# One product's halves in another order, and two ring copies cut in two: a strided-attention and MLP kernel on Trainium2

## The chip, the cores and the metric

The kernel runs on one core of a Trainium2 chip. Its time is the device time of one execution in microseconds; lower is better. The engines go by these names in the profile: PE is TensorE's matmul, PEld its weight load, DVE is VectorE, ACT is ScalarE, POOL is GpSimd, SP is SyncE, which here only issues DMAs. A small q behind a name means that engine's instruction queue.

## The reference: what is computed

Two stages follow each other. The first is attention over 8 batches of 8 heads, 576 positions and 64 values per head, where the heads 0 to 3 see the last 32 positions and the heads 4 to 7 see every 32nd one. The second is an MLP with a leaky activation on the 4608 tokens that come out, with `d_model` 512 and `d_ff` 2048.

```python
scores = scale * np.matmul(q, k.transpose(0, 1, 3, 2))
mask_local = (rel >= 0) & (rel < stride)
mask_strided = (rel >= 0) & (pos[None, :] % stride == pos[:, None] % stride)
scores = np.where(masks[None, :, :, :], scores, -1000000000.0)
attn = softmax(scores)                      # written out in the reference
x = (attn @ v).transpose(0, 2, 1, 3).reshape(B * S, H * D)
h = x @ w_in
g = np.maximum(h, 0.0) + alpha * np.minimum(h, 0.0)
out = g @ w_out
```

## The kernel before, in words

**Tiles and stages.** The 4608 tokens of the MLP are taken in nine chunks of 512 (0 to 8). Attention works on batches of 576 tokens, two heads at a time (a pair: `hp` 0 and 1 are the local heads, 2 and 3 the strided ones). Its results go, transposed, into `xT`, a ring of 1536 columns for the 512 rows of x. A chunk reads 512 columns of the ring; a batch fills 576, so batches and chunks don't end together. Batch 7 fills columns 960 to 1535. Chunk 7 reads columns 512 to 1023, so it needs the first 64 columns of batch 7; chunk 8 reads columns 1024 to 1535.

**How a batch gets into the ring.** Local pairs of later batches go by a transposing DMA from SP's queue straight into `xT` (L446). The strided pair `hp` 2 goes by a transposing DMA into a tile `xs` (L443), and from there by a ScalarE copy that reorders the columns (`x_copy`, L452). The strided pair `hp` 3 is transposed on TensorE into a PSUM tile `xp` (L429) and copied by ScalarE in the same reordering (`x_piece`, L207). `spans` says into which stretches of the ring a batch goes: one, or two where it wraps.

**Layer 1.** For each of 16 groups of 128 rows of `d_ff`, four matmuls of 128x512 (L583) make `hps` in PSUM, in the order 2, 3, 0, 1 of the row blocks of x. ScalarE makes `neg` (L591), VectorE joins both to the activation `gT` (L594). Three PSUM banks are in use for these groups and for the banks of layer 2.

**Layer 2.** From chunk 2 on, the product of `gT` and `w_out` is made with seven products in place of eight (Winograd's form). The 512 tokens are split into two token halves, the columns of `w_out` into two halves, and the contraction over `d_ff` into pairs of 128-row blocks, even and odd. The kernel's products P1 to P7 are made in the order 1, 5, 6, 2, 7, 3, 4. Each is two runs of 8 matmuls of 128x256 (L708): run r makes the r-th 128 tokens of the product's 256, and its step y goes over the eight pairs of `d_ff`. P3, P5, P6 and P7 take sums `gsum` of the four parts of `gT`; P5 takes `gsum[0]`, P6 takes `gsum[1]`, which is made from `gsum[0]`. Each sum is made in two halves by L652: half 0 is pairs 0 to 3 (the first half of `d_ff`), half 1 is pairs 4 to 7. Half 0 of `gsum[0]` and of `gsum[2]` is made early on GpSimd, the rest on VectorE behind the last activations of the chunk. So steps 0 to 3 of P5 need GpSimd's half, and steps 4 to 7 need VectorE's.

**Order.** Every instruction is put out in program order on its engine. The loop at the end of the kernel steps through 30 pieces of a chunk (16 of layer 1, 14 of layer 2) and sets attention pieces of the next batch between them at an even rate. P5 is steps 2 and 3 of layer 2 (its runs r = 0 and r = 1), P6 steps 4 and 5. In chunk 8, the last, the second run of P5 has a PSUM bank of its own. In chunks 7 and 8 there is no attention left to do.

The wait for a sum is carried by the weight load of the first matmul that needs it; what stands behind that load on TensorE waits with it.

Of the kernel before, what the change touches and what calls it, by code (L numbers as in the profile page):

```python
# [32 lines left out]
def kernel(  # L33
# [10 lines left out]
    nc = tc.nc  # L44
    keep = tc.keep_in_program_order

    B, H, S, D = q.shape
# [24 lines left out]
    wsum = [cpool.tile([128, 8, 256], F16, name=f"wsum{i}") for i in range(4)]  # L72
    gsum = [cpool.tile([128, 8, 256], F16, name=f"gsum{i}") for i in range(4)]
# [131 lines left out]
    def cast_copy(eng, o, i):  # L205
        if eng == "act":
            keep(nc.scalar.copy(o, i))  # L207
        elif eng == "dve":
            keep(nc.vector.tensor_copy(o, i))
        else:  # L210
            keep(nc.gpsimd.tensor_copy(o, i))  # L211
# [205 lines left out]
            pvv[:, :, 0:64],  # L417
            rc[0:w, 0:nb].unsqueeze(2).to_broadcast([w, nb, 64]), op=ALU.mult))

    def spans(b):  # L420

        d0 = b * S % RING
        w = min(S, RING - d0)
        return [(0, d0, w)] + ([(w, 0, S - w)] if w < S else [])

    def x_piece(P, eng):
        xp = pspool.tile([128, 1024], F16, tag="ps", name="xp")
        for t in range(P.n):
            keep(nc.tensor.transpose(  # L429
                xp[:, P.w * t : P.w * t + P.w], P.x16[0 : P.w, 128 * t : 128 * t + 128], ident[0 : P.w, 0 : P.w]))  # L430
        for s0, d0, w in spans(P.b):
            o = xT[:, P.hp, d0 : d0 + w]
            if P.strided:
                cast_copy(
                    eng, o.rearrange("r (p t) -> r p t", t=8),
                    xp[:, 0:576].rearrange("r (t p) -> r p t", t=8)[:, s0 // 8 : (s0 + w) // 8, :])
            else:
                cast_copy(eng, o, xp[:, s0 : s0 + w])

    def x_dma(P):  # L440
        if P.strided:
            P.xs = xpool.tile([128, 8, 80], F16, tag="xs", bufs=2, name="xs")
            keep(nc.sync.dma_start_transpose(P.xs, P.x16[0:80, :]))  # L443
        else:
            for s0, d0, w in spans(P.b):
                keep(nc.sync.dma_start_transpose(  # L446
                    xT[:, P.hp, d0 : d0 + w].rearrange("r (w p) -> r w p", p=96),
                    P.x16[0:96, 128 * (s0 // 96) : 128 * ((s0 + w) // 96)]))

    def x_copy(P):  # L450
        for s0, d0, w in spans(P.b):
            keep(nc.scalar.copy(  # L452
                xT[:, P.hp, d0 : d0 + w].rearrange("r (p t) -> r p t", t=8),
                P.xs[:, :, s0 // 8 : (s0 + w) // 8].rearrange("r t p -> r p t")))
# [17 lines left out]
    def X(g, eng=None):  # L472
        return lambda: x_piece(pairs[g], eng or ("act" if pairs[g].strided else "dve"))

    for g in range(7, npair + 2):
# [30 lines left out]
        for i, (kind, fn) in enumerate(seq):  # L506
# [6 lines left out]
            def run(fn=fn, extra=extra, g=g, c=c, kind=kind, lastp=(i == lastP), first=(i == 0),  # L513
# [29 lines left out]
                if second and 4 * DX <= g - 3 < npair and pairs[g - 3].xd and pairs[g - 3].strided:  # L543
                    after.append(lambda: x_copy(pairs[g - 3]))
# [109 lines left out]
    def store(n, t, c, src, add=None, r=None):  # L654

        osb = opool.tile([128, 512], F32, tag="osb", name="osb")
        r0, o = 512 * n + 256 * t, osb
        if r is not None:
            r0, o, src, add = r0 + 128 * r, osb[:, 0:256], src[:, 0:256], add[:, 256 * r : 256 * r + 256]
        if add is None:  # L660
            keep(nc.scalar.copy(o, src))  # L661
        else:
            keep(nc.vector.tensor_tensor(o, src, add, op=ALU.add))  # L663
        dst = out[r0 : r0 + (256 if r is None else 128), 256 * c : 256 * c + 256]
        if r is None:
            dst, o = dst.rearrange("(r p) c -> p r c", p=128), o.rearrange("p (r c) -> p r c", r=2)
        keep(nc.sync.dma_start(dst, o))

    bank = {}

    def lin2_fast(n, i):

        last = n == NCH - 1
        x, r = (("1", i) if i < 2 else ("5", i - 2) if i < 4 else ("6", i - 4) if i < 6 else ("2", i - 6) if i < 8
                else ("7", i - 8) if i < 10 else ("3", i - 10) if i < 12 else ("4", i - 12))
        if last and i > 10:
            x, r = (("4", 0), ("4", 1), ("3", 1))[i - 11]  # L680
        b = {"1": "a", "2": "a", "5": "e", "3": "e"}.get(x, "b")
        first = x in "15" and r == 0
        if first:
            bank[b] = phpool.tile([128, 512], F32, tag="hps", name="ops")
        o = bank[b][:, 256 * r : 256 * r + 256]
        if last and b == "e" and r == 1:
            if x == "5":
                bank["f"] = pspool.tile([128, 512], F32, tag="ps", name="opsl")
                first = True
            o = bank["f"][:, 0:256]  # L690

        def g(t, j):
            return lambda y: gTs[n][:, 2 * y + j, 256 * t + 128 * r : 256 * t + 128 * r + 128]

        def s(z):
            return lambda y: gsum[z][:, y, 128 * r : 128 * r + 128]

        def w(j, c):
            return lambda y: wout16[:, 2 * y + j, 256 * c : 256 * c + 256]

        def t(z):
            return lambda y: wsum[z][:, y, :]

        lhs, rhs = {
            "1": (g(0, 0), w(0, 0)), "2": (g(0, 1), w(1, 0)), "3": (s(3), w(1, 1)),
            "4": (g(1, 1), t(3)), "5": (s(0), t(0)), "6": (s(1), t(1)), "7": (s(2), t(2))}[x]
        for y in range(8):
            keep(nc.tensor.matmul(  # L708
                o, lhs(y), rhs(y), start=(first and y == 0), stop=(y == 7), skip_group_check=True))
        if last and x == "3":  # L710
            store(n, 0, 1, bank["f" if r else "e"], bank["s6"], r)
            return
        if last and x == "5":
            if r == 0:
                bank["s5"] = npool.tile([128, 512], F32, tag="par", bufs=2, name="par")
            keep(nc.scalar.copy(bank["s5"][:, 256 * r : 256 * r + 256], o))
            return
        if r == 0:
            return
        if x == "1":  # L720
            bank["b"] = phpool.tile([128, 512], F32, tag="hps", name="ops")
            keep(nc.scalar.copy(bank["b"], bank["a"]))
        elif x in "56":
            z = npool.tile([128, 512], F32, tag="par", bufs=2, name="par")
            keep(nc.scalar.copy(z, bank[b]))  # L725
            bank["s" + x] = z
        elif x == "2":
            store(n, 0, 0, bank["a"])
        elif x == "7":
            late.append(lambda: store(n, 1, 1, bank["b"], bank["s5"]))  # L730
        elif x == "3":
            late.append(lambda: store(n, 0, 1, bank["e"], bank["s6"]))
        else:
            store(n, 1, 0, bank["b"])
# [173 lines left out]
    for n in range(1, NCH):  # L908
        ab = attn_until(n + 1) if n + 1 < B else len(pieces)
        left = ab - pos["i"]  # L910
        acc = -1.5 if n == 1 else 0.0
        for i in range(32 if n < FAST else 30):
            if i < 16:
                lin1_piece(n, i if n < FAST else 8 * (i // 8) + 2 * (i % 4) + i % 8 // 4)
            elif n < FAST:
                lin2_piece(n, i - 16)
            else:
                lin2_fast(n, i - 16)
            acc += left / (22 if n < FAST else 19.5 if n == B - 2 else 21) * (0.5 if i < 16 else 1.0)
            cnt = int(acc)  # L920
            acc -= cnt
            attn_n(cnt, ab)
            if n < FAST:
                if i in (18, 21, 24, 27):
                    wout_sum((i - 18) // 3)
                continue
            for z, h, eng in sums.get(i, ()):
                g_sum(n, z, h, eng)
        while pos["i"] < ab:
            attn_step(ab)  # L930
# [30 lines left out]
```

## Time and profile before

| what | value |
|---|---|
| time, median of 3 runs | 301.9 us (301.6 to 302.09) |
| the profiled execution's own time | 301.52 us |
| its span, first to last instruction | 299.7 us |
| granted TensorE clock, mean | 0.998 |
| TensorE matmul busy | 293.2 us (98%) |
| VectorE, ScalarE, GpSimd busy | 219.1, 178.6, 171.9 us |
| chunks 3, 4, 5 (123.6 to 214.6 us) | 30.3, 30.3, 30.4 us each |
| chunk 6 (214.6 to 243.8 us) | 29.2 us |
| chunk 7 (243.8 to 270.0 us) | 26.2 us |

All times inside an execution are counted from the start of the span. The profile's waits list an engine's idle time in front of an instruction and what ended it; idle times under 0.15 us are not listed. In a timeline row the first number is the start and the second the length, and a number behind x says how many instructions of a kind the row joins. A matmul's length is longer than the distance to the next one, because matmuls are pipelined. The chain that ended last is followed back from the last instruction: at each step to what released it, or to the instruction before it on its engine.

### The profile page before, as it was taken

Reading aid. Unit: us, or ns where it says so; the run is one execution under the profiler, and the core shown is the slowest. Engines: PE = TensorE matmul, PEld = TensorE weight load, DVE = VectorE, ACT = ScalarE, POOL = GpSimd, SP = SyncE. Lnnn points to the kernel's source line nnn. Section 1 sums busy time; section 2 is a strip of 40 time slices with the busy share of each in tenths; the row PEclk is TensorE's granted clock in tenths of the full one; section 3 lists DMA queues with packets and bytes.
Section 4 is the critical chain, followed back from the end, with each engine's and each line's share of the span. In section 5 each row is a group of like instructions: output and inputs, shape, how many; then the busy total and the mean of one; then the engine's idle time right before and its main releaser. Section 6 shows DMA issues by size and latency. Waiting matters only on the chain.

```text
span 299.7 us, 6824 instructions
## 1 busy us (share of the span) xinstructions
PE 293.2 (98%) x2683; PEld 181.8 (61%) x2683; DVE 219.1 (73%) x408; ACT 178.6 (60%) x330; POOL 171.9 (57%) x160
## 2 busy tenths in 40 slices
PE   8999999999999999999999999999999999999995
PEld 3754545554544478646864686468745964684584
DVE  5677886668775897588848984898489948926852
ACT  1676755698457765776477647764676356416730
POOL 8362270049969998979897987595563305002300
PEclk9999999999999999999999999999999999999999
DMA  7999999999996969999989999966811140022004
GB/s 184 257 191 199 241 211 264 198 209 298 115 204 133 113 101 102 177 178 125 132 147 181 139 150 163 208 95 95 193 22 21 24 140 0 2 72 70 0 2 141
DMA packets 96976, 41.18 MB, mean 137 GB/s; under 512 B 75360, under 2 KB 93232, under 8 KB 96944
## 3 DMA queue, kind: packets, MB, share of 16 engines
q0 software_dynamic: 51008, 17.77, 59.0%
q1 hardware_dynamic: 45584, 22.32, 35.1%
q10 hardware_dynamic: 352, 0.66, 0.9%
q8 instruction: 21, 0.34, 0.5%
q14 instruction: 11, 0.09, 0.1%
HBM read 38.24 MB, written 9.44 MB: 159 GB/s over the span
## 4 chain that ended last, share of the span: by engine, by line
PE 84%; DVE 7%; ACT 4%; issue 2%; DMA 2%; SPq 0%; DVEq 0%; ACTq 0%
PE hps L583 37%; PE ops L708 24%; PE ops L622 5%; PE pv L406 4%; PE ops L864 3%; DVE gsum L652 2%; DVE gT L594 2%; PE sp L353 2%; DMA consts<-consts 2%; ACT neg L591 1%; PE xp L429 1%; PE sph L353 1%; DVE x L415 1%; PE ops L879 1%; ACT et L382 1%
## 5 line engine op out<-in xcount | busy, mean ns | idle before, releaser
L583 PE MATMUL hps<-xT,win 128*128 128x512 f16 x576 | 131.9, 379 | 0.2 <-ACT xT L452 0.2
L594 DVE SCALAR_TENSOR_TENSOR gT<-neg,oma,hps 128x512 f16<-128x512 f32 x144 | 105.3, 744 | 36.5 <-ACT neg L591 28.4
L591 ACT ACTIVATE neg<-hps 128x512 f32<-128x512 f32 x144 | 85.8, 598 | 35.7 <-PE hps L583 33.7
L583 PEld LDWEIGHTS <-win 128*128 128x128 f16 x576 | 53.7, 98 | 59.2 <-issue 0.5
L652 POOL TENSOR_TENSOR gsum<-gT 128x1024 f16<-128x1024 f16 x14 | 29.7, 2123 | 42.2 <-DVE gT L594 37.2
L378 POOL TENSOR_TENSOR et<-et,consts 128x576 f16<-128x576 f16 (+1 forms) x24 | 34.7, 1446 | 30.7 <-ACT et L376 30.5
L708 PEld LDWEIGHTS <-gsum 128*128 128x128 f16 x448 | 40.9, 98 | 7.3 <-DVE gsum L652 1.9
L708 PE MATMUL ops<-wsum,gsum 128*128 128x256 f16 x328 | 41.6, 273 | 0.3
L708 PEld LDWEIGHTS <-gT 128*128 128x128 f16 x336 | 31.5, 98 | 5.4 <-issue 0.3
L415 DVE TENSOR_TENSOR x<-pv,rc 96x384 f16<-96x384 f32 (+2 forms) x62 | 33.0, 532 | 2.1
L385 POOL TENSOR_TENSOR et<-et,consts 128x576 f16<-128x576 f16 (+1 forms) x24 | 31.4, 1309 | 0.0
L406 PEld LDWEIGHTS <-et 72*128 72x128 f16 (+1 forms) x448 | 23.4, 98 | 11.4 <-issue 1.8
L708 PE MATMUL ops<-wout,gT 128*128 128x256 f16 x224 | 27.9, 273 | 0.1
L376 ACT ACTIVATE et<-sp 128x576 f16<-128x576 f32 (+1 forms) x24 | 15.5, 644 | 17.1 <-PE sp L353 17.1
L413 DVE RECIPROCAL rc<-pv 96x6 f32<-96x6 f32 (+2 forms) x80 | 14.7, 183 | 10.6 <-PE pv L406 10.4
L211 POOL COPY vs<-stv 72x1024 f16<-72x1024 f16 x12 | 13.3, 1115 | 15.2 <-DMA stv<-in_v_dram 15.2
L663 DVE TENSOR_TENSOR osb<-ops,par 128x512 f32<-128x512 f32 (+1 forms) x14 | 9.4, 673 | 16.1 <-PE ops L708 8.2
L382 ACT ACTIVATE et<-sph 128x288 f16<-128x288 f32 (+1 forms) x48 | 18.8, 409 | 0.0
L661 ACT COPY osb<-ops 128x512 f32<-128x512 f32 x14 | 8.2, 585 | 16.8 <-PE ops L708 16.7
L622 PE MATMUL ops<-wout,gT 128*128 128x512 f16 x64 | 16.4, 379 | 0.0
L406 PE MATMUL pv<-vs,et 72*128 72x65 f16 x256 | 15.4, 193 | 0.8 <-ACT qT L207 0.5
L725 ACT COPY par<-ops 128x512 f32<-128x512 f32 x13 | 7.6, 585 | 14.1 <-PE ops L708 14.1
(105 smaller groups left out, 331.8 us busy)
## 6 DMA issues: line engine op xcount, KB each, us to landing
out_dram<-osb SPq DMA_DIRECT2D x35, 256.0 KB, 4.0
vl<-in_v_dram POOLq DMA_DIRECT2D x6, 384.0 KB, 9.3
win<-in_moe_w_in_dram POOLq DMA_DIRECT2D x4, 512.0 KB, 17.6
wout<-in_moe_w_out_dram POOLq DMA_DIRECT2D x4, 512.0 KB, 15.6
qsd<-in_q_dram POOLq DMA_DIRECT2D x7, 288.0 KB, 6.2
ksd<-in_k_dram POOLq DMA_DIRECT2D x7, 288.0 KB, 7.6
stv<-in_v_dram POOLq DMA_DIRECT2D x7, 288.0 KB, 7.8
ql<-in_q_dram SPq DMA_DIRECT2D x3, 576.0 KB, 7.3
```

The lines of the kernel that those rows point to most:

```text
L376: keep(nc.scalar.activation(ev.rearrange("r (y c) -> r y c", y=2), sp[0:r, :, 0:n], AF.Exp, scale=SCALE))
L378: keep(nc.gpsimd.tensor_tensor(mv, mv, m, op=ALU.mult))
L382: keep(nc.scalar.activation(ev[:, n * y : n * y + n], sps[y][0:r, 0:n], AF.Exp, scale=SCALE))
L385: keep(nc.gpsimd.tensor_tensor(mv, mv, m, op=ALU.mult))
L406: keep(nc.tensor.matmul(pv[:, 65 * x : 65 * x + 65], et[0:r, c : c + 128], v16[0:r, 2 * P.pr + hh, t, :] if P.strided else v16[:, 6 * (2 * ...
L415: keep(nc.vector.tensor_tensor(P.x16[0:w, c0 : c0 + 64 * nb].rearrange("r (c e) -> r c e", e=64), pvv[:, :, 0:64], rc[0:w, 0:nb].unsqueeze ...
L583: keep(nc.tensor.matmul(hps, win16[:, kk, 128 * m : 128 * m + 128], xT[:, kk, c0 : c0 + 512], start=(kk == 2), stop=(kk == 1)))
L591: keep(nc.scalar.activation(neg, hps, AF.Relu, scale=-1.0))
L594: keep(nc.vector.scalar_tensor_tensor(gTs[n][:, m, :], neg, oma[:, m : m + 1], hps, op0=ALU.mult, op1=ALU.add))
L622: keep(nc.tensor.matmul(ops, gTs[n][:, kf, 128 * mt : 128 * mt + 128], wout16[:, kf, :], start=(kf == 0), stop=(kf == 15)))
L652: keep((nc.vector if eng == "dve" else nc.gpsimd).tensor_tensor(gsum[i][:, hs], a, b, op=op))
L708: keep(nc.tensor.matmul(o, lhs(y), rhs(y), start=(first and y == 0), stop=(y == 7), skip_group_check=True))
```

## The change

There are two parts.

1. P5 of the chunks 2 to 7. Before, run r = 0 goes through the steps 0 to 7 and then run r = 1 through the steps 0 to 7. After, the first of the two pieces takes the steps 0 to 3 of both runs, and the second the steps 4 to 7 of both. The matmuls are the same sixteen, into the same bank. Chunk 8 keeps the old order.
2. Batch 7's strided pairs. `spans` gets an argument; where it is set and the batch is the last, it gives two stretches, 64 and 512 columns long, in place of one of 576. So the copy from `xp` (L207) and the copy from `xs` (L452) become two each. The order on ScalarE is: 64 columns from `xp`, 512 from `xp`, 64 from `xs`, 512 from `xs`. Local pairs and other batches stay.

```diff
-    def spans(b):
+    def spans(b, cut=False):
 
         d0 = b * S % RING
+        if cut and b == B - 1:
+            return [(0, d0, 64), (64, d0 + 64, S - 64)]
         w = min(S, RING - d0)
         return [(0, d0, w)] + ([(w, 0, S - w)] if w < S else [])
...
-        for s0, d0, w in spans(P.b):
+        for s0, d0, w in spans(P.b, P.strided):
...
     def x_copy(P):
-        for s0, d0, w in spans(P.b):
+        for s0, d0, w in spans(P.b, True):
...
+        def both(h):
+            for z in range(2):
+                for y in range(4 * h, 4 * h + 4):
+                    keep(nc.tensor.matmul(
+                        bank["e"][:, 256 * z : 256 * z + 256], gsum[0][:, y, 128 * z : 128 * z + 128], wsum[0][:, y, :],
+                        start=(z == 0 and y == 0), stop=(y == 7), skip_group_check=True))
+
...
-        for y in range(8):
+        if x == "5" and not last:
+            both(r)
+        for y in range(8 if x != "5" or last else 0):
             keep(nc.tensor.matmul(
                 o, lhs(y), rhs(y), start=(first and y == 0), stop=(y == 7), skip_group_check=True))
```

## The prediction

> **What bounds the kernel now.** I read the page first (shares, the chain that ended last), then the table of waits, then the timeline around the waits that the change touches, at last single matmuls in windows of a tenth of a microsecond. The page says TensorE: it is busy for 98% of the span and holds 84% of the chain, so only its idle time can be won. The table of waits then names its two idle times that this change speaks of.
>
> ```profile
> PE 293.2 (98%) x2683; PEld 181.8 (61%) x2683; DVE 219.1 (73%) x408; ACT 178.6 (60%) x330; POOL 171.9 (57%) x160
> PE 84%; DVE 7%; ACT 4%; issue 2%; DMA 2%; SPq 0%; DVEq 0%; ACTq 0%
> PEld L708 <- DVE gsum L652: 1.9, 6, 0.4
> PE hps L583 <- ACT xT L452: 0.2, 1, 0.2
> ```
>
> The first wait is six stalls of the weight loads at P5's fifth matmul, where the second half of its sum is still being made on VectorE: once each in chunks 2, 3, 4, 5, 7 and 8 (chunk 6 has none). The second is the first matmul of chunk 7, which waits for the copy that fills the x ring.
>
> Chunk 3, the timeline of VectorE and of the weight loads (start, length, both us):
>
> ```profile
> 139.66 1.28 POOL L385 TENSOR_TENSOR et<-et,consts 72x576 f16<-72x576 f16 x1
> 140.40 1.10 DVE L652 TENSOR_TENSOR gsum<-gT 128x1024 f16<-128x1024 f16 x1
> 141.43 0.68 DVE L652 TENSOR_TENSOR gsum<-gsum,gT 128x1024 f16<-128x1024 f16 x1
> 142.72 0.68 DVE L652 TENSOR_TENSOR gsum<-gsum,gT 128x1024 f16<-128x1024 f16 x1
> ...
> 141.56 1.21 PEld L708 LDWEIGHTS <-gsum 128*128 128x128 f16 x12 [0.33 <-DVE gsum L652]
> ...
> 142.98 0.35 PEld L708 LDWEIGHTS <-gsum 128*128 128x128 f16 x4
> 143.45 0.11 PEld L708 LDWEIGHTS <-gsum 128*128 128x128 f16 x2
> ```
>
> The sums of VectorE come out at 141.50 (P5's second half), 142.11 and 143.40 (P6's two halves). P5 is held until 141.56. What matters more is the last row: P6's fifth weight load stands at 143.45, 0.05 behind the sum that ends at 143.40. P6 is held too, for a time under the 0.15 us from which the profile lists a wait.
>
> Chunk 7, and its start:
>
> ```profile
> 257.60 1.91 PE L708 MATMUL ops<-wout,gT 128*128 128x256 f16 x16
> 259.67 0.27 PE L708 MATMUL ops<-wsum,gsum 128*128 128x256 f16 x1
> 259.96 0.28 PE L708 MATMUL ops<-wsum,gsum 128*128 128x256 f16 x1
> ...
> 259.82 1.28 DVE L652 TENSOR_TENSOR gsum<-gsum,gT 128x1024 f16<-128x1024 f16 x2
> ...
> 241.89 0.64 ACT L207 COPY xT<-xp 128x576 f16<-128x576 f16 x1 [3.48 <-PE xp L429]
> 242.43 1.31 ACT L452 COPY xT<-xs 128x576 f16<-128x576 f16 x1
> 243.64 0.58 ACT L661 COPY osb<-ops 128x512 f32<-128x512 f32 x1
> 244.85 0.60 ACT L591 ACTIVATE neg<-hps 128x512 f32<-128x512 f32 x1 [0.62 <-PE hps L583]
> ...
> 243.33 0.27 PE L708 MATMUL ops<-wsum,gT 128*128 128x256 f16 x1
> 243.79 0.38 PE L583 MATMUL hps<-xT,win 128*128 128x512 f16 x1 [0.18 <-ACT xT L452]
> ```
>
> Sixteen matmuls in 1.91 us, the last of them 0.27 long, start (1.91 - 0.27) / 15 = 0.109 us apart. The matmuls at 259.67 and 259.96 are P5's fourth and fifth, those at 243.33 and 243.79 the last of chunk 6 and the first of chunk 7; both pairs stand further apart than 0.109.
>
> **P5's order.** It adds and removes no matmul: 16 of 128x256 before and after, six times. Only the order in them and the place of one wait change: the weight load that waits for VectorE is the ninth of P5 in place of the fifth, four matmuls or 0.44 us later. On VectorE, GpSimd and SP the order of all instructions stays, with every DMA issue and queue. What waits behind the held load is the rest of P5 and then all of TensorE's queue, as before. In the new order the bank's halves alternate three times in place of once; in chunk 7 the step from one half, and from one bank, to the next keeps the spacing of 0.109, so I cost it at nothing.
>
> In chunk 7 the fifth matmul starts 259.96 - 259.67 = 0.29 after the fourth in place of 0.109: 0.18 lost. The ninth load would stand at 259.24 + 8 x 0.109 = 260.11, and the sum is out at 259.21 + 0.69 = 259.90: nothing waits. P6 then starts 0.18 sooner; its fifth load would stand at 259.24 + 20 x 0.109 = 261.42, and its sum is out at 261.10: nothing waits there either, and from there to the end the chain is TensorE's. Gain 0.18.
>
> The weight-load rows would say more, 0.29 idle here and 0.36 at chunk 7's start, 0.65 together; I count matmul starts, since weight loads run one slot ahead of their matmuls and that slot costs nothing. The Trainium skill (TensorE: Matmul & The Clock Gate, Part 2) states just this, that the engine pulls weight loads ahead of matmuls in flight; the trace agrees, the fifth load being due at 259.67 for a matmul due at 259.78. By it the sum is the smaller one.
>
> In chunks 2 to 5 P5 loses 110.61 - 110.27 - 0.11 = 0.23 and three times 141.56 - 141.24 - 0.11 = 0.21 (single matmuls in the same windows). Here P6 follows, and its second half is pinned: the VectorE chain that ends at 143.40 runs without idle time, and the one attention product in it was finished on TensorE before P5 began. P5 ends 0.21 sooner, P6's fifth load still starts at 143.45, and all behind it stays. Chunk 2 is the same with 112.84 and 112.89, chunks 4 and 5 repeat chunk 3. Gain 0, between 0 and 0.23 + 3 x 0.21 = 0.86, if the pin were not there. I take 0, because the row at 143.45 shows the pin in the trace of before. Chunk 6 had no stall, chunk 8 keeps the old order.
>
> **The copies.** Batch 7 takes columns 960 to 1535 of the ring; chunk 7 needs only the first 64 of them, chunk 8 the rest. Two ScalarE copies become four. The rows by shape give what a copy takes until the next starts: 0.54 us for 576 columns (241.89 to 242.43), and from the copies of other batches 0.37 for 384 and 0.21 for 192, so about 0.05 + 0.00085 per column: 0.10 for 64, 0.48 for 512. The strided ones last 0.58, 0.95 and 1.32 for 192, 384 and 576: about 0.2 + 0.0019 per column, so 0.33 for 64. The small strided copy then runs from 241.89 + 0.10 + 0.48 = 242.47 to 242.80. TensorE asks for it at 243.33 + 0.109 = 243.44, so it is hidden with 0.6 to spare. Even if the 64 columns took the whole 0.58 of the 192-column row, it ends at 243.05. The first matmul starts at 243.44 in place of 243.79. Gain 0.35; the bounds are 0 and 0.35, and I take the upper one.
>
> What is late next: ScalarE's queue is longer by some 0.12 us, two fixed parts of 0.05 to 0.06. Its store copy (L661) starts at about 243.76 and ends at 244.35; the first relu of chunk 7 asks for ScalarE at 244.85 - 0.35 = 244.50, and the third group of matmuls, which takes that copy's bank, at 245.16. Both are covered, by 0.15 and 0.8.
>
> **The sum.** 0.18 + 0.35 = 0.53 us, all in front of or in chunk 7, after which no engine but TensorE sets the end. The profiled execution took 301.52 (its span 299.7 and 1.8 around it), so it would take 300.99; the median of the runs, 301.9, is 0.38 above that execution, and I forecast against it: 301.37, 0.18% less. A change of 0.2%, 0.6 us, is about what a measurement of this kernel can tell from none; the forecast lies just inside.
>
> **The rivals.**
> 1. All of P5's stalls are won. If the second sums came out sooner too, chunks 2 to 5 would give their 0.86: 301.9 - 0.53 - 0.86 = 300.51. For it: in chunk 3 the first sum takes 1.10, in chunk 7 the same sum 0.69, so 0.41 of VectorE's delay is no work of its own; it overlaps the GpSimd multiplication of 139.66 to 140.94, and without that both sums would be out before P5 and P6 ask. Against: the change moves nothing on GpSimd or VectorE. The Trainium skill (SBUF — State Buffer, Who interferes with whom) has that as a lock: a VectorE operation with two SBUF inputs and a GpSimd one block each other, whoever starts first. The trace agrees with 1.10 against 0.69. Chance 0.07.
> 2. P5 alone pays; the start of chunk 7 stays held by something that stands just behind the copy. 301.9 - 0.18 = 301.72. For it: the copies' source comes by a transposing DMA issued at 237.46, of a kind that takes 3.4 in the median, and another execution may have it later than 242.43; against: in this one it was there. Chance 0.10.
> 3. The copies alone pay, P5's 0.18 being lost again at P6's first half: 301.55. Against: 0.3 of slack in the rows above. Chance 0.08.
> 4. Neither moves the end, because the wait stays with the whole copy: 301.9. Against: in the changed program's order the ninth load carries the wait, and the matmul waits for the third of the four copies. Chance 0.03.
> 5. Slower: ScalarE's small copies. Bound each new copy by the whole one it is cut from, 0.64 + 1.31 = 1.95 more: the store copy ends at 246.18, the first relu starts 1.58 late, and the fourth group of matmuls, which needs the first group's bank (three banks), waits about 1.5: 301.9 - 0.53 + 1.5 = 302.9. It decides from the point where the queue is 0.83 later than I price it (0.15 of cover before the relu, 0.15 behind it, and the gain of 0.53); for 0.2% slower it needs 1.4. Against: 192 columns cost 0.58, not 1.31. Chance 0.06.
>
> **How the numbers follow.** The forecast has 0.66. The three runs of before lie 0.5 apart, and the forecast is only 0.07 inside the bound, so a little under half of its chance (0.32) would read as faster by over 0.2%; with rival 1 and a bit of rival 3 that is 0.40. Slower by over 0.2% is most of rival 5 and some scatter, 0.06. Within 0.2% is the rest, 0.54. The range goes from 300.7, which leaves out most of rival 1, to 302.0, which takes in rivals 2 to 4 and leaves out rival 5: about 0.15 outside. The forecast's own range is 301.1 to 301.6.
>
> **What will show it.** In the changed kernel's trace: no wait of weight loads for VectorE's sum in chunk 7, and chunk 7's first matmul 0.11 behind chunk 6's last; four copies in ScalarE's rows, the small strided one about 0.33 long; chunk 7 shorter by 0.18. In chunks 2 to 5 the listed wait should not vanish but stand at P6, at 0.2 to 0.4 each, with the length of these chunks unchanged. I am wrong if chunks 2 to 5 get shorter (rival 1), if the first matmul of chunk 7 still waits (rival 2), or if a matmul group of chunk 7 waits for ScalarE (rival 5).

## The result, and the profile after

The changed kernel takes 301.19 us (median of 22 runs, 300.94 to 301.63); the kernel before, run beside it on the same chip, 301.81 us. The ratio is 0.9981, with a 95% interval of 0.9974 to 0.9988: by the ratio 0.57 us faster (the two medians lie 0.62 apart), for the 0.53 that was forecast. The whole interval lies below 1, so the kernel is faster; whether by more than 0.2% stays open.

One profiled execution of each can be compared chunk by chunk. A chunk's length here is the distance from its first layer-1 matmul to the next chunk's, read from single matmuls of the timeline (chunk 8: to the start of the last matmul, 3.45 before the end of both spans). The chunks in the table of before are cut at round times, so chunk 6 has 29.2 there and 29.38 here.

| us | before | after |
|---|---|---|
| start of chunk 1 | 57.34 | 57.59 |
| chunk 2 | 31.47 | 31.51 |
| chunks 3, 4, 5 | 30.31, 30.31, 30.32 | 30.34, 30.32, 30.33 |
| chunk 6 (ends with the ring copies) | 29.38 | 29.03 |
| chunk 7 | 26.23 | 26.04 |
| chunk 8 | 26.24 | 26.25 |
| span | 299.70 | 299.50 |

Chunk 6 has won 0.35 and chunk 7 0.19, both as forecast; chunks 2 to 5 have won nothing. The span shows only 0.20 of it, because this execution's start was 0.25 late. The instructions up to there are the same in both kernels, and over all the profiles of this study chunk 1 starts between 57.29 and 57.72.

The page after, in the lines shown of before (busy time by engine; the chain that ended last):

```profile
PE 293.3 (98%) x2683; PEld 182.7 (61%) x2683; DVE 219.0 (73%) x408; ACT 179.1 (60%) x332; POOL 171.9 (57%) x160
...
PE 85%; DVE 7%; ACT 3%; issue 3%; DVEq 0%; ACTq 0%
```

The waits of weight loads after, whole span (total, times, longest):

```profile
PEld L719 <- DVE gsum L654: 1.8, 6, 0.4
```

1.8 us and six times, where before had 1.9 and six: by this row the waits for sums have hardly changed, though they now stand elsewhere, two in chunk 2 and one each in chunks 3, 4, 5 and 8. (L719 is now the line of P6 and of chunk 8's P5; P5's new order is L709, and it has no wait in the list.) The other row, matmuls that waited for the ring copy, is gone. Where P5's stall went is seen in chunk 3, on VectorE and among the weight loads:

```profile
140.69 1.12 DVE L654 TENSOR_TENSOR gsum<-gT 128x1024 f16<-128x1024 f16 x1
141.74 0.68 DVE L654 TENSOR_TENSOR gsum<-gsum,gT 128x1024 f16<-128x1024 f16 x1
...
143.03 0.68 DVE L654 TENSOR_TENSOR gsum<-gsum,gT 128x1024 f16<-128x1024 f16 x1
...
143.29 0.10 PEld L719 LDWEIGHTS <-gsum 128*128 128x128 f16 x1
143.76 0.22 PEld L719 LDWEIGHTS <-gsum 128*128 128x128 f16 x3 [0.37 <-DVE gsum L654]
```

P6's fifth load waits 0.37 for the sum that ends at 143.71 and starts 0.05 behind it, as it did before. P5's stall has become P6's. In the chain of chunk 7 the copies and the pauses are gone (start, length, what; a row starts where the chain passes to it, which can be a little after its first matmul):

```profile
242.18 1.75 PE ops L719 x16
243.93 13.81 PE hps L585 x64
257.75 1.75 PE ops L719 x16
259.49 1.75 PE ops L709 x16
261.24 0.76 PE ops L719 x7
```

From chunk 6's last product to the end of chunk 7, TensorE follows itself without a break. The four copies on ScalarE, each row joining a small one and a large one:

```profile
242.22 0.70 ACT L207 COPY xT<-xp 128x64 f16<-128x64 f16 x2 [3.48 <-PE xp L431]
242.81 1.41 ACT L454 COPY xT<-xs 128x64 f16<-128x64 f16 x2
244.10 0.60 ACT L663 COPY osb<-ops 128x512 f32<-128x512 f32 x1
244.83 0.60 ACT L593 ACTIVATE neg<-hps 128x512 f32<-128x512 f32 x1
```

The small strided copy, seen in a window of its own, lasts 0.33 and is done at 243.14; TensorE's first matmul of chunk 7 starts at 243.77, in its turn. The store copy comes 0.13 later than it would have, and the first relu is not held.

### The profile page after: what moved, and what is told of

Its sections match the earlier page's. It is cut to its first block, busy times and chain, and to the rows that moved or that the text cites. A ratio compares the mean times of both kernels' runs of the same rounds, so it can differ in the third digit from the quotient of the medians.

```text
span 299.5 us, 6826 instructions
## 1 busy us (share of the span) xinstructions
PE 293.3 (98%) x2683; PEld 182.7 (61%) x2683; DVE 219.0 (73%) x408; ACT 179.1 (60%) x332; POOL 171.9 (57%) x160
## 4 chain that ended last, share of the span: by engine, by line
PE 85%; DVE 7%; ACT 3%; issue 3%; DVEq 0%; ACTq 0%
PE hps L585 37%; PE ops L719 22%; PE ops L624 5%; PE pv L406 4%; PE ops L875 3%; PE wps L761 3%; DVE gsum L654 2%; DVE gT L596 2%; PE sp L353 2%; ACT neg L593 1%; PE xp L431 1%; PE sph L353 1%; PE ops L890 1%; PE ops L709 1%; ACT et L382 1%
## 5 line engine op out<-in xcount | busy, mean ns | idle before, releaser
L719 PEld LDWEIGHTS <-gsum 128*128 128x128 f16 x352 | 32.2, 98 | 5.8 <-DVE gsum L654 1.8
L719 PEld LDWEIGHTS <-gT 128*128 128x128 f16 x336 | 31.5, 98 | 5.4 <-issue 0.3
L719 PE MATMUL ops<-wsum,gsum 128*128 128x256 f16 x232 | 30.2, 273 | 0.3
L406 PEld LDWEIGHTS <-et 72*128 72x128 f16 (+1 forms) x448 | 23.4, 98 | 11.3 <-issue 1.4
L719 PE MATMUL ops<-wout,gT 128*128 128x256 f16 x224 | 27.9, 272 | 0.1
L406 PE MATMUL pv<-vs,et 72*128 72x65 f16 x256 | 15.4, 193 | 0.9 <-ACT qT L207 0.5
```

Source lines behind the costliest of these rows:

```text
L406: keep(nc.tensor.matmul(pv[:, 65 * x : 65 * x + 65], et[0:r, c : c + 128], v16[0:r, 2 * P.pr + hh, t, :] if P.strided else v16[:, 6 * (2 * ...
L719: keep(nc.tensor.matmul(o, lhs(y), rhs(y), start=(first and y == 0), stop=(y == 7), skip_group_check=True))
```

## The experiments

Line numbers of layer 2 in the profiles below differ by a few from kernel to kernel. The first theory was the prediction's: two gains that have nothing to do with each other, and chunks 2 to 5 pinned by P6's second sum. All timed runs are compared with the kernel before on the same chip.

### The copies alone, P5 alone, and one copy alone

`e1_copies` takes the changed kernel and puts P5 back:

```diff
-        if x == "5" and not last:
-            both(r)
-        for y in range(8 if x != "5" or last else 0):
+        for y in range(8):
```

> The cut copies alone, P5 in its old order. Theory (two independent gains): 0.35 us faster than before, ratio 0.9988; chunk 6, counted from its first layer-1 matmul to chunk 7's, goes from 29.38 to 29.03 us, and chunk 7 keeps 26.23 with its P5 stall of 0.29 between two matmul starts. Rival (the gain of the change is P5's, the copies are hidden anyway): ratio 1.000 and chunk 6 at 29.38.

`e2_p5` keeps P5's order and takes the cut away:

```diff
-        if cut and b == B - 1:
+        if False:
```

> P5's new order alone, the copies whole. Theory (P6's second sum pins chunks 2 to 5): 0.18 us faster than before, ratio 0.9994, too little for a verdict by time; in the trace chunk 7 goes from 26.23 to 26.05 and chunks 2 to 5 keep their 31.5, 30.3, 30.3, 30.3. Rival (all of P5's stalls are won): chunks 2 to 5 shorter by 0.2 each, 1.0 us in all, ratio 0.9966.

`e3_xs_cut` is `e1_copies` with the copy out of `xp` whole again:

```diff
-        for s0, d0, w in spans(P.b, P.strided):
+        for s0, d0, w in spans(P.b):
```

> Only the strided copy out of xs is cut, the copy out of xp stays whole, P5 in its old order. Theory (what held chunk 7 was the 1.31 us of the strided copy): the whole 0.35 us, ratio 0.9988, chunk 6 at 29.03. The small copy then ends at about 242.43 + 0.33 = 242.76 on the old trace, 0.7 before TensorE asks. Rival (both cuts are needed): chunk 6 stays between 29.1 and 29.4, ratio above 0.999.

| | ratio to before, 95% | chunk 6 | chunk 7 | chunks 2 to 5 |
|---|---|---|---|---|
| e1_copies | 0.9990 (0.9981 to 0.9999) | 29.03 | 26.23 | 31.47, 30.32, 30.30, 30.31 |
| e2_p5 | 0.9990 (0.9982 to 0.9999) | 29.38 | 26.04 | 31.47, 30.31, 30.30, 30.31 |
| e3_xs_cut | 0.9989 (0.9980 to 0.9998) | 29.03 | 26.23 | 31.49, 30.31, 30.30, 30.31 |

The times can hardly tell 0.2 from 0.35 us; the chunk lengths can. In all thirteen profiles of this study chunk 6 takes 29.38 with the strided copy whole and 29.03 or 29.04 with it cut, and chunk 7 takes 26.23 with P5's old order and 26.04 with the new one. Each part does its own piece and nothing else, the parts add up, and P5's order gives nothing in chunks 2 to 5. Of the four copies only the small strided one is needed: with the `xp` copy whole the gain is the same 0.35.

### Does P6's sum pin chunks 2 to 5?

`e4_p5_p6` gives P6 the same order, so that its ninth matmul asks for its second sum, and not its fifth. The expectation counts this as 0.44 us. In chunks 3 to 5 the scores also stand between P6's two pieces, and it is 0.9 us (143.26 and 144.15 in chunk 3 of `e9_sums_behind` below, where nothing waits there):

```diff
+            k = "56".index(x)
             for z in range(2):
                 for y in range(4 * h, 4 * h + 4):
                     keep(nc.tensor.matmul(
-                        bank["e"][:, 256 * z : 256 * z + 256], gsum[0][:, y, 128 * z : 128 * z + 128], wsum[0][:, y, :],
-                        start=(z == 0 and y == 0), stop=(y == 7), skip_group_check=True))
+                        bank[b][:, 256 * z : 256 * z + 256], gsum[k][:, y, 128 * z : 128 * z + 128], wsum[k][:, y, :],
+                        start=(k == 0 and z == 0 and y == 0), stop=(y == 7), skip_group_check=True))
...
-        if x == "5" and not last:
+        if x in "56" and not last:
             both(r)
-        for y in range(8 if x != "5" or last else 0):
+        for y in range(8 if x not in "56" or last else 0):
```

> The changed kernel, and P6 in the same order as P5 (first half of d_ff for both token halves, then the second) in chunks 2 to 7. Theory (in chunks 2 to 5 the stall only moved to P6's second sum): P6 now asks for that sum 0.44 us later, and chunks 3, 4 and 5 give 0.2 us each; chunk 2 gives little, since an attention product behind P6 waits for VectorE there. 0.65 us faster than the changed kernel, 1.2 faster than before, ratio 0.9961. Rival (something else sets the pace of these chunks, VectorE as a whole or attention): chunks 3 to 5 keep 30.3 us and the ratio is that of the changed kernel, 0.998.

The theory failed. The ratio is 0.9984 (0.9975 to 0.9993), and chunks 3 to 5 take 30.33, 30.32, 30.32. P6 no longer waits in them. What does stands in this kernel's waits of weight loads in chunks 3 to 5 (total, times, longest):

```profile
PEld L353 <- DVE x16s L415: 0.6, 3, 0.2
```

and in its timeline of weight loads in chunk 3:

```profile
143.76 0.20 PEld L353 LDWEIGHTS <-kT 64*128 64x128 f16 x7 [0.21 <-issue]
144.17 0.15 PEld L353 LDWEIGHTS <-kT 64*128 64x128 f16 x5 [0.22 <-DVE x16s L415]
```

An attention product here is VectorE's scaling of finished attention sums, from PSUM into the tile `x16s`; three of them stand among the sums of chunk 3. The scores behind P6's first piece need a PSUM bank that the second of them (143.56 to 144.11) still reads. So the stall moved a second time, and its size stayed: 0.24 between two score matmuls, and 0.12 more at the next attention matmuls (`pv`, L406). That leaves two readings: the order of work on VectorE is unlucky, or VectorE's total in this stretch is too long and TensorE pays at whatever it comes to next.

`e8_sum_later` tells them apart. It moves P6's second sum behind that product; chunk 8's P5 is in halves too, as in `e5_last` below.

```diff
...
-        16: [(1, 1, "dve")], 18: [(2, 1, "dve")], 19: [(3, 0, "dve")], 20: [(3, 1, "dve")]}
+        17: [(1, 1, "dve")], 18: [(2, 1, "dve")], 19: [(3, 0, "dve")], 20: [(3, 1, "dve")]}
```

> P5 and P6 in halves as in the run before that had both, chunk 8's P5 in halves, and on VectorE the second half of P6's sum one piece later, so that it stands behind the second attention product and not ahead of it. In the run without that, the stall of chunks 3 to 5 stood at the scores, which wait for the PSUM bank of that product until 144.1. Theory (the order on VectorE decides, its total does not): the product comes out at 143.4, the scores start without a wait at 143.8, P6's second half comes behind them and finds its sum at 144.0; chunks 3, 4 and 5 lose 0.2 to 0.3 us each, chunk 8 0.19; ratio to before 0.9950 to 0.9958. Rival (VectorE's total in this stretch sets the pace, and TensorE waits for it at whichever place comes next): chunks 3 to 5 stay within 0.1 of 30.3 and the ratio is that of the kernel with chunk 8's halves alone, 0.9975.

Ratio 0.9972 (0.9961 to 0.9984), chunks 3 to 5 at 30.32, 30.30, 30.31. The second product did come out earlier and the scores did not wait; the stall moved a third time, to the attention matmuls behind P6. Matmuls that waited in chunks 3 to 5:

```profile
PE pv L406 <- DVE x16s L415: 0.6, 3, 0.2
```

These matmuls are where all the orders meet. In chunk 3 of before, VectorE's third attention product and the `pv` matmuls that take its PSUM bank:

```profile
144.81 0.42 DVE L415 TENSOR_TENSOR x16s<-pv,rc 72x256 f16<-72x256 f32 x1
...
145.38 0.34 PE L406 MATMUL pv<-vs,et 72*128 72x65 f16 x6
```

They start 0.15 after the product is done, and lose 0.12, too little for the list of waits. In before, after, `e1_copies` to `e4_p5_p6`, `e5_last` and `e8_sum_later` alike, in each of the chunks 3 to 5, this product is done 21.76 to 21.80 us after the chunk's first matmul, the `pv` matmuls start 0.15 behind it, and the chunk ends 8.39 after that. From the last activation to this product VectorE has no idle time in the list.

So the rival holds for all orders tried so far: VectorE's total between the last activation and the third attention product sets the length of these chunks, and the place where TensorE stands still is the only thing that these edits change.

### What makes VectorE's stretch long

The prediction's first rival had named the candidate: P5's second half takes 1.10 us here and 0.69 in chunk 7, where GpSimd does nothing beside it. Two kernels leave out GpSimd's mask multiplication over the second half of a strided pair's scores, one with P5's new order and one with the old:

```diff
-                if y:
+                if y and not P.strided:
                     keep(nc.gpsimd.tensor_tensor(mv, mv, m, op=ALU.mult))
```

> The changed kernel without GpSimd's mask multiplication over the second half of a strided pair's scores (that part of the mask is left out). Theory (VectorE's first sum is long because GpSimd reads at the same time): the sum takes 0.7 in place of 1.1 us in chunks 3 to 5, P6's sums come out 0.4 sooner, and these chunks go from 30.3 to about 30.1. Rival (the sum is long for another cause, or VectorE is late by other work): the sum keeps 1.1 us and the chunks 30.3.

> The kernel before without the same multiplication. Theory: P5's second half comes out at about 0.4 us sooner, in time for the fifth matmul of the old order; P5's listed wait goes in chunks 3 to 5, and these chunks take the same as in the changed kernel without the multiplication, about 30.1. Rival: the old order keeps a stall there and stays 0.2 longer than the new one.

VectorE in chunk 3 of `e6_after_no_mask`:

```profile
140.13 0.69 DVE L654 TENSOR_TENSOR gsum<-gT 128x1024 f16<-128x1024 f16 x1
140.74 0.69 DVE L654 TENSOR_TENSOR gsum<-gsum,gT 128x1024 f16<-128x1024 f16 x1
...
142.03 0.68 DVE L654 TENSOR_TENSOR gsum<-gsum,gT 128x1024 f16<-128x1024 f16 x1
```

The first sum takes 0.69. From its start to the end of P6's second sum there are now 2.58 us (140.13 to 142.71), where the changed kernel needs 3.02 (140.69 to 143.71). Chunks 2 to 5 take 30.93, 29.93, 29.93, 29.93 with the new order and 30.93, 29.93, 29.93, 29.93 with the old. The listed waits for sums are gone in chunks 3 to 5 of both. One run of each took 300.01 and 300.58 us. That is 0.38 per chunk in chunks 3 to 5, where about 0.2 was expected and P5's own stall was 0.22, and it makes P5's order worthless there: without the delay the old order does not wait. Leaving the multiplication out also frees GpSimd, so this pair alone does not show that the overlap is what costs.

### Filling the time instead

`e9_sums_behind` leaves nothing out. P5 (all chunks) and P6 (chunks 2 to 7) are in halves, and the sums stand one piece later on VectorE. So the first attention product stands ahead of P5's second half, while GpSimd multiplies, and the second ahead of P6's. In these lines (shown against the changed kernel) `e8_sum_later` differs from it by the 15 alone:

```diff
...
-        5: [(2, 0, "pool")], 9: [(0, 0, "pool")], 15: [(0, 1, "dve"), (1, 0, "dve")],
-        16: [(1, 1, "dve")], 18: [(2, 1, "dve")], 19: [(3, 0, "dve")], 20: [(3, 1, "dve")]}
+        5: [(2, 0, "pool")], 9: [(0, 0, "pool")], 16: [(0, 1, "dve"), (1, 0, "dve")],
+        17: [(1, 1, "dve")], 18: [(2, 1, "dve")], 19: [(3, 0, "dve")], 20: [(3, 1, "dve")]}
```

> P5 and P6 in halves in chunks 2 to 7, P5 also in chunk 8, and on VectorE the sums one piece later: the first attention product stands ahead of P5's second half, the second ahead of P6's. Theory (the 0.41 us by which P5's sum is long is VectorE standing still while GpSimd reads, and that is what these chunks pay): the product reads PSUM, fills that time, and the sum behind it takes 0.7 us; VectorE is through with the stretch 0.4 us sooner, and chunks 3, 4 and 5 go from 30.31 to between 29.95 and 30.1, one of the sums being late for P5 by 0.4 on the way; ratio to before 0.993 to 0.995. Rival (the product in front only delays the sums, and TensorE waits at P5 what it saves later): 30.3, ratio 0.997.

`e10_sums_behind_p5` has the same order on VectorE with P6 in its old order:

> The same order on VectorE, with P5 alone in halves (all chunks) and P6 in its old order. Theory: P6's fifth matmul asks before the second product and the sum behind it are done, so a part of the gain stays at P6: chunks 3, 4 and 5 between 30.0 and 30.3, ratio to before 0.994 to 0.997. Rival: as for the run with P6 in halves, 30.3 or more, ratio 0.997 or above.

`e11_p5_old` is `e9_sums_behind` with P5 in its old order in chunks 2 to 7:

```diff
-        if x == "5" or x == "6" and not last:
+        if x == "5" and last or x == "6" and not last:
             both(r)
...
```

> The fastest kernel so far (sums one piece later, P5 and P6 in halves), with P5 back in its old order in chunks 2 to 7. The question: with VectorE's stretch no longer the pace, is P5's order worth something in chunks 3 to 5? If it is: the fifth matmul of the old order, due at about 141.25 on that trace, waits for the sum that ends at 141.70, 0.5 us, and chunks 3 to 5 go from 29.93 to between 30.1 and 30.4. If it is not, because P6's halves alone carry it: 29.93 to 30.0.

`e9_sums_behind` takes 299.68 us, ratio 0.9927 (0.9915 to 0.9940), the fastest of the study; the gain is a little above what the theory gave. Its chunks 2 to 8 take 31.38, 29.93, 29.93, 29.93, 29.03, 26.04 and 26.05. GpSimd and VectorE in its chunk 3:

```profile
139.71 1.28 POOL L385 TENSOR_TENSOR et<-et,consts 72x576 f16<-72x576 f16 x1
...
140.33 0.18 DVE L413 RECIPROCAL rc<-pv 72x6 f32<-72x6 f32 x1
140.55 0.55 DVE L415 TENSOR_TENSOR x16s<-pv,rc 72x384 f16<-72x384 f32 x1
141.02 0.68 DVE L654 TENSOR_TENSOR gsum<-gT 128x1024 f16<-128x1024 f16 x1
141.62 0.68 DVE L654 TENSOR_TENSOR gsum<-gsum,gT 128x1024 f16<-128x1024 f16 x1
...
142.44 0.55 DVE L415 TENSOR_TENSOR x16s<-pv,rc 72x384 f16<-72x384 f32 x1
142.92 0.68 DVE L654 TENSOR_TENSOR gsum<-gsum,gT 128x1024 f16<-128x1024 f16 x1
```

The product runs beside the multiplication in its usual 0.55, and the sum behind it takes 0.68. All the work is there, and chunks 3 to 5 are as short as with the multiplication left out. Against `e8_sum_later` only the place of two sums is another. This shows that the overlap of the sum with GpSimd's multiplication is what these chunks paid for. In chunk 2 two sums still meet GpSimd's multiplications and take 1.16 and 1.76 us, so that chunk wins only 0.1.

Both halves are needed for it. With P6 in its old order (`e10_sums_behind_p5`) the ratio is 0.9989 (0.9980 to 0.9998), outside what the theory gave it and as its rival had it: chunk 2 takes 31.93 and chunks 3 to 5 30.33, the old length. With P5 in its old order (`e11_p5_old`, one run, 300.95 us) they take 30.31, 30.30, 30.31, in the range expected if P5's order is worth something there. One stall each, weight loads of chunk 3, first of `e10_sums_behind_p5`:

```profile
144.16 0.22 PEld L718 LDWEIGHTS <-gsum 128*128 128x128 f16 x3 [0.50 <-DVE gsum L654]
```

and of `e11_p5_old`:

```profile
141.68 0.55 PEld L719 LDWEIGHTS <-gsum 128*128 128x128 f16 x6 [0.48 <-DVE gsum L654]
```

Between matmul starts these two cost 0.39 and 0.37. They are not the old wait: the third attention product is now done 0.7 us before its `pv` matmuls start, and holds nothing. In their old order P6 and P5 ask for their sums that much before they are out. That this comes to nearly the 0.38 that VectorE had saved is, as far as the traces show, a coincidence.

### Chunk 8

`e5_last` is the changed kernel with chunk 8's P5 in halves (the lines that give the second token half its own bank are left out):

```diff
...
-        if x == "5" and not last:
+        if x == "5":
             both(r)
...
         if last and x == "5":
-            if r == 0:
+            if r == 1:
                 bank["s5"] = npool.tile([128, 512], F32, tag="par", bufs=2, name="par")
-            keep(nc.scalar.copy(bank["s5"][:, 256 * r : 256 * r + 256], o))
+                keep(nc.scalar.copy(bank["s5"][:, 0:256], bank["e"][:, 0:256]))
+                keep(nc.scalar.copy(bank["s5"][:, 256:512], o))
```

> The changed kernel, and chunk 8's P5 in the new order too (its two PSUM banks are filled in turn, both ScalarE copies of P5 follow at the end). Chunk 8 has no attention beside it, as chunk 7. Both theories, the pin by P6's sum and the pace of VectorE among attention work, expect the same here as in chunk 7: chunk 8, from its first layer-1 matmul to the last matmul, goes from 26.24 to 26.05, 0.19 us faster than the changed kernel, ratio to before 0.9975.

Ratio 0.9972 (0.9962 to 0.9982), chunk 8 at 26.06, 0.19 shorter, as expected. The gain in a chunk without attention repeats.

## Why the prediction was right, point by point

- **P5 in chunk 7, 0.18.** Measured 0.19, alone (`e2_p5`) and in the changed kernel. Counting matmul starts and not the idle time of weight loads was right: that row said 0.29.
- **P5 in chunks 2 to 5, nothing.** Measured 0.00 to 0.01 alone, and 0.01 to 0.04 longer in the one profile of the changed kernel. The forecast that the wait would stand at P6 with 0.2 to 0.4 held: 0.37 in chunk 3. The reason given for it was only half of it. P6's sum is the first of three places where TensorE runs into VectorE there; taking it away (`e4_p5_p6`) moved the stall to the scores, and then (`e8_sum_later`) to the `pv` matmuls behind P6. What pins these chunks is VectorE's whole stretch up to its third attention product. P6's sum was enough to forecast that P5's new order wins nothing; it was not enough to forecast the next edit, and `e4_p5_p6`, planned on it, missed.
- **The first rival.** Its mechanism, the sum held by GpSimd's multiplication, is real and the change does not touch it, as was said. Its price was too small: 0.86 us counted P5's stalls alone. `e6_after_no_mask` against the changed kernel gives 0.58 in chunk 2 and 0.39 to 0.41 in each of the others, 1.8 in all, because the later waits for VectorE go with it. With GpSimd's work kept, `e9_sums_behind` gives the same in chunks 3 to 5. The prediction did not look at the `pv` matmuls behind P6, which lose 0.12 us to VectorE in the trace of before.
- **The copies, 0.35.** Measured 0.35. The small strided copy took 0.33, as worked out from the three other sizes; the store copy came 0.13 late for 0.12 said, and the relu was covered. That the other cut is not needed (`e3_xs_cut`) was in the same rows, since the strided copy would have ended at 242.76 behind a whole one too; the prediction didn't ask.
- **The rivals 2 to 5** did not come: each part paid by itself, and no matmul of chunk 7 waits for ScalarE.
- **The size.** Forecast 0.18%, measured 0.19%, with an interval of 0.12% to 0.26%. The time alone would also fit a gain of 0.4 or 0.7 us; that both terms were right is shown by the lengths of chunks 6 and 7.

## What to carry to other kernels

A wait that is removed from the bound engine is won only as far as nothing else that it needs later from the same partner engine is late too; follow the partner engine to the end of its backlog, not to the next wait. A weight load's idle time in these profiles is one matmul slot longer than what the matmuls lose (0.29 against 0.18 in chunk 7), so price stalls by the distance of matmul starts. Where two engines slow each other, look for an operation of the slowed one that does not take part, and put it in that time: here that, with the halves of P6 and of chunk 8, took 2.2 us off the kernel before, where the change took 0.57, and only then did the new order of products pay in the chunks with attention.

## What was unexpected in the hardware

A VectorE sum of two 128x1024 half-precision operands in SBUF takes 0.68 alone and 1.09 to 1.12 in chunks 3 to 5, where it starts beside a GpSimd multiplication that keeps its 1.28; in chunk 3 of before the two overlap by 0.54 and the sum loses 0.42. An operation with one operand in PSUM and one small one in SBUF, in the same place, keeps its 0.55. The Trainium skill (SBUF — State Buffer, Who interferes with whom) gives both: two SBUF inputs block, fewer do not; the runs agree.

The price can also fall on GpSimd. Later in chunk 3 of before, two sums keep 0.68 each, and the multiplication beside them takes 2.44, where the same one alone takes 1.27 to 1.29:

```profile
145.13 2.44 POOL L378 TENSOR_TENSOR et<-et,consts 128x576 f16<-128x576 f16 x1 [1.29 <-ACT et L376]
145.16 1.28 DVE L652 TENSOR_TENSOR gsum<-gT,gsum 128x1024 f16<-128x1024 f16 x2
```

That costs nothing here: in `e9_sums_behind` this multiplication still takes 2.16, and no wait of TensorE for GpSimd is listed in that chunk. The prediction did not ask about the order on VectorE, which was worth 1.1 us over three chunks.

Three edits that took one stall of TensorE away each left chunks 3 to 5 at 30.30 to 30.34 us, to within 0.04. A chunk length that does not move while its waits do is a sign of a pace set elsewhere. It is no proof: `e10_sums_behind_p5` and `e11_p5_old` come to 30.30 to 30.33 too, by stalls of their own.
